# Summing three operands instead of four in phases 4 to 9 of an attention-and-MoE kernel, with the joined additions shared by VectorE and GpSimd

## The chip, the cores and the metric

One Trainium2 chip, one core. The metric is the device time of one execution in microseconds (us); before the change the median of three runs is 819.66 us (819.66 to 819.79).

## What is computed

A clustered attention is followed by two feed-forward layers. Queries and keys of 2 x 8 heads (768 rows of 64) are each assigned to the nearest of 16 centroids; a query sees the keys of its own cluster alone.

```python
mask = q_assign[:, :, :, None] == k_assign[:, :, None, :]
scores = scale * np.matmul(q, k.transpose(0, 1, 3, 2))
scores = np.where(mask, scores, -1000000000.0)
scores = scores - np.max(scores, axis=-1, keepdims=True)
attn = np.exp(scores)
attn = attn / (np.sum(attn, axis=-1, keepdims=True) + 1e-09)
return np.matmul(attn, v).astype(np.float32)
```

The result, 1536 rows of 512, goes through `h = x @ w_in` (512 to 2048) with a leaky rectifier and `@ w_out`, and then through a gated layer with RMS normalization (512 to 1536 and back). The change touches the attention alone: the sum over the keys in the denominator, and how one operand of the scores is split.

## The kernel before

**Phases and slots.** The attention is done by pairs of heads (`pr`, 0 to 7). Each pair has two phases (`ph`, 0 to 15), one for each half of its 768 queries; a phase has six slots, one for each tile of 128 keys, so that phase `ph` starts at slot 6 ph. In a slot TensorE makes the scores of 128 keys x 384 queries for both heads (`st_tile`, L712 and L713, transposed: keys lie on the partitions), and ScalarE takes their exponential into a tile P of 128 x 2 x 384 (L714). Every second slot, `pv_tiles` multiplies the last two tiles with the values (L728).

**The denominators.** They are sums of P over the keys, hence over partitions, and so a product with a matrix of ones into the bank `ps_sm` (L739): four small matmuls per tile of P, one for each head and half of the queries, each into 32 rows of the bank. A fp32 matmul stands in the trace as two entries, so that one operand is 8 entries of L739. In phases 4 to 12 (`SUMMED`) TensorE doesn't sum all six tiles of P: VectorE adds the first two and the next two (`pair_add`, L747, 128 x 768), and the last call of `pv_tiles` in the phase, at the slot after its end, sums what is in the list `adds` and the last two tiles of P. That is four operands. In the phases of the table `WHOLE`, 10 and 11 before the change, `pair_join` (L751) also adds the two sums to one, so that three operands are left; there the joined one is taken last (`q = P + self.adds`), elsewhere the additions come first.

**The maxima, nine slots ahead.** For the softmax, the score product is also made with queries on the partitions (`max_tile`, L662), in two halves into the single banks `ps_ma` and `ps_mb`, each reduced by VectorE to one column (L664). TensorE may write a bank again when VectorE has reduced it. At the end of a phase's six tiles the maxima of the two halves are joined (L681) and split in a rounded part and the rest (L671, L672, `max_split`); TensorE turns them into rows (`max_rows`, L690), and ScalarE copies these into the operand of the scores (L699).

**Preparing the pairs.** For each pair, some 40 slots ahead and by the tables `PAIR`, `FIFTH` and so on (slots counted from the pair's first one, 12 pr): squares of q and k (L469), their sums (L483), the norms by three Newton steps (`prep_norm`, L435 to L442, VectorE, tiles of 128 x 24), similarities and argmax (L543 to L565), and the split of q and k in a rounded part (`hi`, L606, ScalarE, 128 x 768) and a residual (`lo`, L614: for q by VectorE, for k of pairs 4 to 7 by GpSimd). The pairs 0 to 4 have tables of their own; `FIFTH` (pair 4) takes `hi` from `PAIR` and has a `lo` of its own.

**The output of a phase.** One to twelve slots after its end: reciprocals (L757 to L769), their split by GpSimd (L774, L775), the product X (L787, VectorE), its rounding (`x1h`, L795, ScalarE) and its residual (`x1l`, L798, GpSimd). The weights of the feed-forward layers are decoded in the same slots from slot 59 on.

**What sets the order.** `plan` puts every step into a slot with a number that orders it inside the slot, and `slot` issues the steps of a slot in that order. So each engine has a fixed queue and no step overtakes another on its engine; between engines only the data's waits count. `at(s, o, fn, ...)` is the call: slot, number, step.

```python
def at(s, o, fn, *a):
    ev.setdefault(s, []).append((o, len(ev.get(s, [])), fn, a))
```

Of the kernel before, what the change touches and what calls it, by code (L numbers as in the profile page):

```python
# [13 lines left out]
ALU = mybir.AluOpType  # L14
# [9 lines left out]
    "sq": ((-38, 4), (-36, 1.015)),  # L24
    "ss": ((-37, 0.6), (-36, 2.05)),
    "norm": tuple((t, 5 + n / 100) for n, t in enumerate([-32] + [-31] * 6 + [-30] * 7)),
    "hi": ((-28, 1.06), (-27, 1.06)),
    "lo": ((-24, 2.3), (-25, 1.05)),
    "sims": ((-30, 1.6), (-29, 1.7)),
    "scale": ((-29, 1.75),),  # L30
    "arg": ((-27, 5), (-24, 2.1), (-24, 2.2), (-22, 1.62), (-21, 5)),
# [57 lines left out]

SUMMED = range(4, 13)  # L90
FULL = (4, 6, 8, 10)
WHOLE = {10: (6, 1.99), 11: (5, 0.59)}
SQUARED = 2
ASIDE = (2,)
NEWTON = (2, 3)
# [130 lines left out]
class Attention:  # L226
# [489 lines left out]
    def pv_tiles(self, u):  # L716
# [13 lines left out]
        if ph in SUMMED and t0 < T - 2:  # L730
            self.addends[u] = P
            return
        q = P + self.adds if ph in WHOLE else self.adds + P
        self.adds = []
# [11 lines left out]
        self.adds.append(a)  # L746
        self.nc.vector.tensor_tensor(out=a, in0=P[0], in1=P[1], op=ALU.add)  # L747

    def pair_join(self):
        a, b = self.adds  # L750
        self.nc.vector.tensor_tensor(out=a, in0=a, in1=b, op=ALU.add)  # L751
        self.adds = [a]

    def out_first(self, ph):
# [45 lines left out]
    def plan(self):  # L800
# [3 lines left out]
        def at(s, o, fn, *a):  # L804
            ev.setdefault(s, []).append((o, len(ev.get(s, [])), fn, a))
# [4 lines left out]
        for pr in range(self.NP):  # L810
            b = SLOTS * pr
# [24 lines left out]
        for ph in range(NF):  # L836
            b = T * ph
            last = ph == NF - 1
            slots = AHEAD.get(ph, [b + k - LEAD for k in range(T)])
            for k, s in enumerate(slots):  # L840
                early = s < 0 or s % 2 and (s > 15 or ph < DIRECT and (s == 15 or slots.count(s) > 1))
                if s >= STEADY and not early:
                    at(s, 1.01, self.max_tile, ph, k, (0,))
                    at(s, 1.03, self.max_tile, ph, k, (1,))
                else:
                    at(s, 2.7 if s in slots[:k] else 0.5 if early else 1.5, self.max_tile, ph, k)
            mid, end = slots[T // 2 - 1], slots[-1]
            if ph < DIRECT:
                at(mid, 1.6, self.max_split, ph, 0)
                at(mid + 1 if ph else mid + 2, 1.8 if ph else 0.6, self.max_rows, ph, 0)  # L850
                last_rows = 1.01 if ph == DIRECT - 1 else 0.7
                at(end, 1.45 if end % 2 and end > 0 else 1.6, self.max_split, ph, 1)
                at(end + 1, last_rows, self.max_rows, ph, 1)
            else:
                at(end, 1.6, self.max_split, ph, None)
                at(end + 1, 0.7, self.max_rows, ph, None)
                at(end + 1, 0.71, self.rows_copy, ph, (0,))
                at(end + 1, 1.01, self.rows_copy, ph, (1,))
            for t in range(T):
                for e in range(2):  # L860
                    ahead = ((-7, 0.6), (-7, 0.7), (-5, 1))[t] if ph == e == 0 and t < 3 else ()
                    at(*(ahead or (b + t, 1 + e / 50)), self.st_tile, b + t, e)
                if t % 2:
                    at(b + t + 1, 2, self.pv_tiles, (b + t) // 2)
                    if ph in SUMMED and t < T - 1:
                        late = ph in FULL and t == 1
                        at(b + t + 1 + late, 1.1 if late else 2, self.pair_add, (b + t) // 2)
            if ph in WHOLE:
                at(b + WHOLE[ph][0], WHOLE[ph][1], self.pair_join)
            calm = STEADY <= b + 7 and not last  # L870
            at(b + (7 if calm else 6), 0.6 if calm else 3, self.out_first, ph)
            at(b + 6, 2.1, self.out_evac, ph)
            at(b + 7, -0.5 if last else 1.025, self.out_recip, ph)
            at(b + 7, -0.4 if last else 1.75, self.out_parts, ph)
            at(b + (8 if last else 10), -0.3 if last else 1.7, self.out_bcast, ph)
            at(b + (8 if last else 10), -0.2 if last else 1.75, self.out_mult, ph)
            soon = ph % 2 == 0 and ph < NF - 2
            at(b + (8 if last else 11 if soon else 12), -0.1 if last else 0.9 if soon else 1.04, self.out_split, ph, 0)
            at(b + (8 if last else 11 if soon else 12), 0 if last else 0.95 if soon else 1.05, self.out_split, ph, 1)
# [495 lines left out]
```

## Time and profile before

| | |
|---|---|
| Median of 3 runs | 819.66 us (819.66 to 819.79) |
| The profiled execution, its time | 819.63 us |
| Its span, from the first to the last instruction | 817.9 us |
| TensorE matmul (PE) | 809.6 us busy, 99% of the span |
| VectorE (DVE) | 623.7 us, 76% |
| ScalarE (ACT) | 335.6 us, 41% |
| GpSimd (POOL) | 362.1 us, 44% |
| TensorE clock granted | 1.0 of full speed in every slice |

The attention takes roughly the first 260 us; phases 4 to 9 lie between 92 and 176 us. They fill the fifth to the ninth of the page's forty slices, and VectorE's busy digit is 9 in each of these; in the second half of the kernel it falls to 7 and below. A busy time counts an instruction from start to end, so that neighbours overlap by some 0.08 us on VectorE and by half of their length on TensorE; what an instruction costs its queue is read from one start to the next. The idle time in brackets is the engine's own, with the instruction that ended it.

### The profile page before, as it was taken

The page shows a single profiled execution, that of the slowest core. Times are in us where ns is not written, and L with a number is a line of the kernel's source. Part 1 is how long each engine was busy: PE and PEld are TensorE (multiplying, and loading weights), DVE is VectorE, ACT ScalarE, POOL GpSimd, SP SyncE. Part 2 cuts the span into 40 slices and gives each one's busy share as a digit, 9 for nine tenths or more (in the row PEclk, how much of TensorE's full clock was granted, in tenths as well). Part 3 has the DMA queues.
Part 4 walks back from the last instruction along what each step waited for, and adds up shares of the span by engine and source line. Part 5 has one row for each costly group of instructions (what it writes and reads, how often), then busy time and mean ns, then how long its engine had stood idle before and what let it go on. Part 6 is the DMA issues. An engine that isn't in the chain of part 4 may idle for free.

```text
span 817.9 us, 11705 instructions
## 1 busy us (share of the span) xinstructions
PE 809.6 (99%) x4350; PEld 625.0 (76%) x4350; DVE 623.7 (76%) x1036; ACT 335.6 (41%) x652; POOL 362.1 (44%) x335
## 2 busy tenths in 40 slices
PE   8999999999999999999999999999999999999998
PEld 5565666666666888888888888888888888888887
DVE  6989999999998489999999977877555555555523
ACT  7655776666564333433434444432212221222110
POOL 3421221221213267786766772416465546554511
PEclk9999999999999999999999999999999999999999
DMA  8786655754532022232212220102121212121012
GB/s 206 201 229 181 132 154 161 171 111 115 133 114 79 1 77 78 78 103 65 88 59 75 77 78 1 51 1 78 52 77 54 76 52 77 57 73 51 1 52 103
DMA packets 23624, 74.03 MB, mean 91 GB/s; under 512 B 3600, under 2 KB 4752, under 8 KB 23568
## 3 DMA queue, kind: packets, MB, share of 16 engines
q1 hardware_dynamic: 23568, 73.29, 31.3%
q8 instruction: 34, 0.56, 0.3%
q14 instruction: 22, 0.18, 0.1%
HBM read 49.88 MB, written 3.15 MB: 65 GB/s over the span
## 4 chain that ended last, share of the span: by engine, by line
PE 96%; DVE 2%; DMA 1%; ACT 1%; issue 0%; SPq 0%; DVEq 0%; ACTq 0%
PE ps_st L1010 35%; PE ps_mx L1010 14%; PE ps_pv L1010 14%; PE ps_pv L728 8%; PE ps_pr L1010 5%; PE ps_st L712 4%; PE ps_st L713 4%; PE ps_sm L739 3%; PE ps_ma L662 3%; PE ps_mb L662 2%; DMA nat<-in_kn_dram 1%; DVE mx L666 1%; PE ps_pv L393 1%; PE ps_pr L516 1%; PE ps_pr L690 0%; PE ps_pr L782 0%
## 5 line engine op out<-in xcount | busy, mean ns | idle before, releaser
L1077 POOL TENSOR_TENSOR gl<-v,gh 128x512 fp32r<-128x512 f32 x68 | 96.0, 1412 | 143.8 <-ACT gh L1076 142.4
L1076 ACT CAST gh<-v 128x512 fp32r<-128x512 f32 x68 | 42.3, 622 | 151.9 <-DVE v L1073 83.3
L1073 DVE TENSOR_TENSOR v<-ps_st,t 128x512 f32<-128x512 f32 x36 | 24.9, 691 | 100.3 <-PE ps_st L1010 100.2
L714 ACT ACTIVATE p<-ps_st 128x384 f32<-128x384 f32 x192 | 85.3, 491 | 28.1 <-PE ps_st L713 26.6
L992 DVE SCALAR_TENSOR_TENSOR dec_a<-raw,dec_a 128x512 uint32<-128x512 uint32 x66 | 81.6, 1236 | 2.2
L728 PE MATMUL ps_pv<-p,vnat 128*64 128x384 f32 x384 | 72.6, 499 | 0.0
L1069 DVE SCALAR_TENSOR_TENSOR v<-v,alpha,t 128x512 f32<-128x512 f32 x45 | 53.0, 1177 | 21.9 <-ACT v L1068 21.8
L712 PE MATMUL ps_st<-op 128*128 128x384 f32 x192 | 67.8, 353 | 0.3 <-ACT oht L575 0.3
L1010 PE MATMUL ps_st<-x1h,stage 128*128 128x512 f32 x272 | 67.2, 389 | 0.0
L713 PE MATMUL ps_st<-op 82*128 82x384 f32 x192 | 65.0, 339 | 0.0
L1010 PEld LDWEIGHTS ps_st<-x1h,stage 128*128 128x128 f32 x272 | 51.1, 188 | 10.6
L1123 DVE TENSOR_TENSOR x<-ps_mx,x 128x1024 f32<-128x1024 f32 x36 | 43.9, 1220 | 18.7 <-PE ps_mx L1010 18.7
L664 DVE TENSOR_REDUCE mx<-ps_ma 128x1 f32<-128x384 f32 x90 | 49.7, 552 | 10.1 <-PE ps_ma L662 9.2
L798 POOL TENSOR_TENSOR x1l<-X,x1h 128x384 fp32r<-128x384 f32 x15 | 15.9, 1062 | 91.7 <-ACT x1h L795 91.7
L1010 PE MATMUL ps_st<-x1h,wvh 128*128 128x512 f32 x144 | 56.2, 390 | 0.0
L1010 PE MATMUL ps_st<-x1h,wvl 128*128 128x512 f32 x144 | 56.0, 389 | 0.0
L1010 PE MATMUL ps_st<-x1h,wih 128*128 128x512 f32 x132 | 51.6, 391 | 0.0
L1010 PE MATMUL ps_st<-x1h,wil 128*128 128x512 f32 x132 | 51.4, 389 | 0.0
L664 DVE TENSOR_REDUCE mx<-ps_mb 128x1 f32<-128x384 f32 x90 | 49.4, 549 | 0.1
L1123 DVE TENSOR_TENSOR x<-ps_pv,x 128x1024 f32<-128x1024 f32 x35 | 42.5, 1214 | 6.8 <-PE ps_pv L1010 6.8
L990 DVE TENSOR_SCALAR dec_a<-raw 128x512 uint32<-128x512 uint32 x66 | 47.6, 722 | 0.0
L995 DVE SCALAR_TENSOR_TENSOR dec_e<-raw,dec_e 128x512 f32<-128x512 uint32 x66 | 45.7, 692 | 2.3
(304 smaller groups left out, 1998.3 us busy)
## 6 DMA issues: line engine op xcount, KB each, us to landing
raw<-in_moe_w_out_dram SPq DMA_DIRECT2D x28, 512.0 KB, 3.5
op<-stage SPq DMA_DIRECT2D x32, 384.0 KB, 5.9
raw<-in_moe_w_in_dram SPq DMA_DIRECT2D x15, 512.0 KB, 3.6
raw<-in_moe_w_val_dram SPq DMA_DIRECT2D x12, 512.0 KB, 3.4
raw<-in_moe_w_gate_dram SPq DMA_DIRECT2D x12, 512.0 KB, 3.4
op<-stage SPq DMA_DIRECT2D x16, 288.0 KB, 5.9
raw<-in_qt_dram SPq DMA_DIRECT2D x8, 384.0 KB, 4.8
raw<-in_kt_dram SPq DMA_DIRECT2D x8, 384.0 KB, 5.1
```

What stands on the lines that cost most here:

```text
L664: nc.vector.tensor_reduce(out=mx[:, g, k:k + 1], in_=to, op=ALU.max, axis=AX.X)
L712: nc.tensor.matmul(ps, lhsT=o1[:, 1, ks], rhs=o1[:, 0, qs], start=True, stop=False)
L713: nc.tensor.matmul(ps, lhsT=o2[:, 1, ks], rhs=o2[:, 0, qs], start=False, stop=True)
L714: nc.scalar.activation(out=self.P[s][:, e], in_=ps, func=AF.Exp, scale=self.scale)
L728: nc.tensor.matmul(ps[64 * e:64 * e + 64], lhsT=self.vnat[ph // 2][:, e, t0 + y], rhs=P[y][:, e], start=t0 + y == 0, stop=t0 + y == T - 1)
L990: lambda: v.tensor_scalar(out=a, in0=top, scalar1=3, scalar2=0x3FFFFFFF, op0=ALU.logical_shift_left, op1=ALU.bitwise_and),
L992: lambda: v.scalar_tensor_tensor(out=a, in0=top, scalar=0xC0000000, in1=a, op0=ALU.bitwise_and, op1=ALU.bitwise_or),
L995: lambda: v.scalar_tensor_tensor(out=ef, in0=bot, scalar=2.0 ** -52, in1=ef, op0=ALU.mult, op1=ALU.mult),
L1010: self.nc.tensor.matmul(ps, lhsT=a, rhs=b, start=first and i == 0, stop=last and i == len(terms) - 1)
L1069: nc.vector.scalar_tensor_tensor(out=v, in0=v, scalar=self.nalpha[:, a], in1=t, op0=ALU.mult, op1=ALU.add)
L1077: nc.gpsimd.tensor_tensor(out=lo, in0=v, in1=f(hi), op=ALU.subtract)
L1123: nc.vector.tensor_tensor(out=dst, in0=ps, in1=dst, op=ALU.add)
```

## The change

Three tables and one step change.

- `WHOLE` gets the phases 4 to 9: in the even ones the join stands in the phase's sixth slot with the number 5, in the odd ones in the fifth slot with 2.5, right after the second `pair_add`. The denominators of these phases are then summed over three operands, the joined one last.
- `pair_join` takes the phase: in phases 5, 7 and 9 GpSimd adds, in the others VectorE.
- `hi` in `PAIR` (pairs 4 to 7): the second rounding, that of k, goes from slot -27 to slot -28, right behind the first.
- `lo` in `PAIR` (pairs 5 to 7): GpSimd's residual of k goes from slot -25 to slot -27.

```diff
--- before.py
+++ after.py
@@ -24,8 +24,8 @@
     "sq": ((-38, 4), (-36, 1.015)),
     "ss": ((-37, 0.6), (-36, 2.05)),
     "norm": tuple((t, 5 + n / 100) for n, t in enumerate([-32] + [-31] * 6 + [-30] * 7)),
-    "hi": ((-28, 1.06), (-27, 1.06)),
-    "lo": ((-24, 2.3), (-25, 1.05)),
+    "hi": ((-28, 1.06), (-28, 1.07)),
+    "lo": ((-24, 2.3), (-27, 0.9)),
     "sims": ((-30, 1.6), (-29, 1.7)),
     "scale": ((-29, 1.75),),
     "arg": ((-27, 5), (-24, 2.1), (-24, 2.2), (-22, 1.62), (-21, 5)),
@@ -89,7 +89,7 @@
 
 SUMMED = range(4, 13)
 FULL = (4, 6, 8, 10)
-WHOLE = {10: (6, 1.99), 11: (5, 0.59)}
+WHOLE = {**{ph: ((5, 5), (4, 2.5))[ph % 2] for ph in range(4, 10)}, 10: (6, 1.99), 11: (5, 0.59)}
 SQUARED = 2
 ASIDE = (2,)
 NEWTON = (2, 3)
@@ -746,9 +746,9 @@
         self.adds.append(a)
         self.nc.vector.tensor_tensor(out=a, in0=P[0], in1=P[1], op=ALU.add)
 
-    def pair_join(self):
+    def pair_join(self, ph):
         a, b = self.adds
-        self.nc.vector.tensor_tensor(out=a, in0=a, in1=b, op=ALU.add)
+        (self.nc.gpsimd if ph % 2 and ph < 10 else self.nc.vector).tensor_tensor(out=a, in0=a, in1=b, op=ALU.add)
         self.adds = [a]
 
     def out_first(self, ph):
@@ -866,7 +866,7 @@
                         late = ph in FULL and t == 1
                         at(b + t + 1 + late, 1.1 if late else 2, self.pair_add, (b + t) // 2)
             if ph in WHOLE:
-                at(b + WHOLE[ph][0], WHOLE[ph][1], self.pair_join)
+                at(b + WHOLE[ph][0], WHOLE[ph][1], self.pair_join, ph)
             calm = STEADY <= b + 7 and not last
             at(b + (7 if calm else 6), 0.6 if calm else 3, self.out_first, ph)
             at(b + 6, 2.1, self.out_evac, ph)
```

How it moves the instructions, first on VectorE at the end of phase 4 (L664 reduces the maxima, L437 and L429 are Newton steps of pair 5; one piece of the difference):

```order
 L664 TENSOR_REDUCE mx<-ps_ma 128x1
 L664 TENSOR_REDUCE mx<-ps_mb 128x1
+L751 TENSOR_TENSOR add_1414<-add_1414,add_1447 128x768
 L437 TENSOR_SCALAR n_y<-n_a 128x24
 L429 TENSOR_TENSOR n_a<-n_y,ss_1280 128x24
```

The join goes in between the reductions and the Newton steps; the same piece comes again in phases 6 and 8.

On GpSimd, from the output steps of phase 4 to those of phase 6, before (L775 splits reciprocals, L798 is the residual of an output, L614 the residual of k of pair 5):

```order
L775 TENSOR_TENSOR hl<-rs,hl 128x192
L798 TENSOR_TENSOR x1l<-X,x1h 128x384
L614 TENSOR_TENSOR stage_106<-raw_1237,stage_106 128x768
L774 TENSOR_SCALAR hl<-rs,low 128x192
L775 TENSOR_TENSOR hl<-rs,hl 128x192
```

and with the change:

```order
L775 TENSOR_TENSOR hl<-rs,hl 128x192
L614 TENSOR_TENSOR stage_106<-raw_1237,stage_106 128x768
L751 TENSOR_TENSOR add_1584<-add_1584,add_1637 128x768
L798 TENSOR_TENSOR x1l<-X,x1h 128x384
L774 TENSOR_SCALAR hl<-rs,low 128x192
L775 TENSOR_TENSOR hl<-rs,hl 128x192
```

The residual of k now stands ahead of the output's, with the join behind it; so in the phases 7 and 9 as well.

On TensorE, the sum of phase 4, before (L728 is the product with the values, L516 belongs to the similarities):

```order
L516 MATMUL ps_pr<-raw_1237,cb 32x384 x4
L728 MATMUL ps_pv<-p,vnat 64x384 x4
L739 MATMUL ps_sm<-add_1414,ones 32x192 x4
L739 MATMUL ps_sm<-add_1447,ones 32x192 x4
L739 MATMUL ps_sm<-p,ones 32x192 x8
L662 MATMUL ps_ma<-op_3_118 128x384
```

and with the change:

```order
L516 MATMUL ps_pr<-raw_1237,cb 32x384 x4
L728 MATMUL ps_pv<-p,vnat 64x384 x4
L739 MATMUL ps_sm<-p,ones 32x192 x8
L739 MATMUL ps_sm<-add_1414,ones 32x192 x4
L662 MATMUL ps_ma<-op_3_118 128x384
```

Four matmuls go, and the tiles of P come ahead of the joined sum.

## Rows read from the trace of the kernel before

**Rows 1.** The page: the chain that ended last, share of the span by engine.

```profile
PE 96%; DVE 2%; DMA 1%; ACT 1%; issue 0%; SPq 0%; DVEq 0%; ACTq 0%
```

**Rows 2.** The chain's pieces, sums of phases 4, 6, 10: start, duration, engine, tile, line, count.

```profile
104.70 1.44 PE ps_sm L739 x32
...
132.92 1.44 PE ps_sm L739 x32
...
188.15 1.11 PE ps_sm L739 x24
```

**Rows 3.** Timeline, VectorE, phase 4's end: start, duration, engine, line, operation [idle before <-releaser].

```profile
102.47 0.18 DVE L431 SCALAR_TENSOR_TENSOR n_y<-n_a,n_y 128x24 f32<-128x24 f32 x1
...
103.94 0.41 DVE L431 SCALAR_TENSOR_TENSOR n_y<-n_a,n_y 128x24 f32<-128x24 f32 x1
...
106.55 0.56 DVE L664 TENSOR_REDUCE mx<-ps_ma 128x1 f32<-128x384 f32 x1 [0.78 <-PE ps_ma L662]
```

**Rows 4.** Timeline, VectorE and TensorE, last slot of phase 6.

```profile
129.12 0.56 DVE L664 TENSOR_REDUCE mx<-ps_ma 128x1 f32<-128x384 f32 x1
...
129.73 0.44 PE L662 MATMUL ps_ma<-op 80*128 80x384 f32 x1
...
130.01 0.34 PE L712 MATMUL ps_st<-op 128*128 128x384 f32 x1
```

**Rows 5.** Timeline, VectorE, third slot of phase 5 (slot 32).

```profile
109.92 0.17 DVE L671 TENSOR_SCALAR mh<-mx 128x6 fp32r<-128x6 f32 x1
110.12 0.17 DVE L672 SCALAR_TENSOR_TENSOR mh<-mx,mh 128x6 fp32r<-128x6 f32 x1
110.21 0.95 DVE L747 TENSOR_TENSOR add<-p 128x768 f32<-128x768 f32 x1
111.08 0.55 DVE L664 TENSOR_REDUCE mx<-ps_ma 128x1 f32<-128x384 f32 x1
```

**Rows 6.** Timeline, GpSimd, phases 2, 4 and 9.

```profile
74.42 1.00 POOL L798 TENSOR_TENSOR x1l<-X,x1h 128x384 fp32r<-128x384 f32 x1 [11.27 <-ACT x1h L795]
...
103.31 1.00 POOL L798 TENSOR_TENSOR x1l<-X,x1h 128x384 fp32r<-128x384 f32 x1 [7.83 <-ACT x1h L795]
...
172.34 1.82 POOL L614 TENSOR_TENSOR stage<-raw,stage 128x768 fp32r<-128x768 f32 x1
```

**Rows 7.** Timeline, VectorE, phase 2.

```profile
74.46 1.00 DVE L429 TENSOR_TENSOR n_a<-n_y,ss 128x24 f32<-128x24 f32 x1
75.49 0.18 DVE L430 SCALAR_TENSOR_TENSOR n_a<-n_a,n_y 128x24 f32<-128x24 f32 x1
...
77.82 0.30 DVE L442 RECIPROCAL n_a<-n_y 128x24 f32<-128x24 f32 x1
78.04 0.49 DVE L664 TENSOR_REDUCE mx<-ps_ma 128x1 f32<-128x384 f32 x1
```

**Rows 8.** Timeline, TensorE, slots 32 and 33.

```profile
108.10 0.34 PE L712 MATMUL ps_st<-op 128*128 128x384 f32 x1
...
110.61 0.34 PE L690 MATMUL ps_pr<-idr,mh 128*64 128x128 f32 x3
...
111.90 0.34 PE L662 MATMUL ps_ma<-op 80*128 80x384 f32 x1
```

**Rows 9.** Timeline, ScalarE, slots 32 and 33.

```profile
109.04 0.82 ACT L606 CAST stage<-raw 128x768 fp32r<-128x768 f32 x1
110.99 0.47 ACT L699 CAST op<-ps_pr 2x384 fp32r<-2x384 f32 x1 [1.13 <-PE ps_pr L690]
...
112.88 0.82 ACT L606 CAST stage<-raw 128x768 fp32r<-128x768 f32 x1
113.60 0.87 ACT L714 ACTIVATE p<-ps_st 128x384 f32<-128x384 f32 x2
```

**Rows 10.** Timeline, VectorE, phase 9.

```profile
173.70 0.87 DVE L555 TENSOR_TENSOR sims<-sims,am 128x384 f32<-128x384 f32 x1
...
176.48 0.56 DVE L664 TENSOR_REDUCE mx<-ps_ma 128x1 f32<-128x384 f32 x1 [0.45 <-PE ps_ma L662]
```

## The prediction

> **What bounds the kernel now.** I read the chain that ended last first: TensorE carries 96% of it [rows 1], so time is saved only where TensorE is given less to do and nothing makes it wait. Then I read the stretch of phases 4 to 9 engine by engine, to see how close VectorE runs behind. Phases come in pairs of 28.2 us (the sums of phases 4 and 6 start at 104.70 and 132.92) [rows 2]. VectorE stops once in a pair for long: 0.78 us before a maximum, after the sums of the even phase [rows 3]. And at one place in a pair TensorE already waits for VectorE: the reduction from 129.12 ends at 129.68, the next score product for ps_ma starts at 129.73, and the matmul behind it at 130.01 [rows 4]. So both engines are nearly full, and what matters is how far VectorE falls behind, not its average.
>
> **The sums.** A sum over four operands takes 1.44 us of the chain, one over three 1.11 us [rows 2]; six phases go from four to three: 6 x 0.33 = 1.98 us less for TensorE. The joined operand now comes last, so it is needed some 0.7 us later than the first. That is the whole gain: 819.63 - 1.98 = 817.65 if nothing waits.
>
> **The joins on VectorE (phases 4, 6, 8).** None stands there in the trace, but the same operation on the same shape does: from a pair's addition at 110.21 to the reduction behind it at 111.08, 0.87 us [rows 5]. The join goes in after the reductions of the phase's last slot, ahead of the Newton steps. The idle 0.78 us after the sums [rows 3] nearly covers it: alone it makes VectorE 0.1 us late.
>
> But it also moves the Newton steps by 0.87 us, and this I charge. The L431 that starts at 102.47 then starts at 103.34. GpSimd's residual of the output (L798) runs from 103.31 to 104.31 [rows 6], since ScalarE sets when, not VectorE. What happens then stands in phase 2: L429 started at 74.46, 0.04 us behind an L798 from 74.42, and took 1.00 us in place of 0.18, to the end of L798 [rows 6, 7]. Now L798 meets only the end of this stretch: L431 at 103.94 took 0.41 us, to 104.35 [rows 3]. So after the join the blocked step again ends at about 104.35, but with more still behind it. L430 then starts at about 104.6; from L430 to the reduction after the last Newton step phase 2 needs 78.04 - 75.49 = 2.55 us [rows 7]. That reduction starts at 107.15, not 106.55: VectorE is 0.60 us late, while TensorE is 0.33 us early. Bounds: 0.1 us late without the block; 0.9 us if L798 is waited for in full (0.1 + 1.00 - 0.23, the wait of L431 that goes away).
>
> **What TensorE does with it.** The reduction of 107.15 ends at 107.71, and the second matmul from there, as in [rows 4], starts 0.33 us after that: 108.04, against 108.10 before [rows 8]. The first saving is spent here, but for 0.06 us.
>
> **The second rounding (ScalarE).** It moves ahead of the copies of the maxima's rows, into 1.13 us in which ScalarE waits for TensorE; one rounding takes 0.72 us to the next start, 0.82 us in all [rows 9]. It costs ScalarE nothing. It would end at 109.04 - 0.06 + 0.72 + 0.82 = 110.52.
>
> **GpSimd's residual sooner (pairs 5 to 7, phases 5, 7, 9).** It now stands ahead of the join and of L798 in GpSimd's queue and takes 1.82 us [rows 6] as soon as that rounding is done, from 110.52 to 110.60. VectorE is then at the splitting of the maxima: L671 at 109.92 + 0.60 = 110.52, L672 at 110.72, the addition at 110.81 [rows 5]. The addition is long and would keep GpSimd out until its end, which would do no harm. But GpSimd asks before that: it comes in when L671 ends (110.69) and runs to 112.51. L672 has two inputs in SBUF, as L431 and L429 have, and a longer one, L555 at 173.70, was held up by just this residual (0.87 us, for 0.55, beside the one from 172.34) [rows 6, 10]. So L672 ends at 112.55, and the matmuls that turn the maxima (L690, 110.61 before [rows 8]) start at 112.6: TensorE stands for 2.0 us with nothing else in its queue. The addition is late by 2.3 us and holds up the next reduction; the product at 111.90 [rows 8] waits 0.1 us for it. So a pair costs between 2.0 us (TensorE) and 2.3 us (VectorE); I take 2.15. The second saving, of the odd phase, is lost where TensorE waits for VectorE already [rows 4].
>
> The Trainium skill (SBUF — State Buffer, "Who interferes with whom") says that a VectorE instruction with two SBUF inputs contends with a GpSimd instruction that reads SBUF, and that the first takes the port pair for all of its instruction. By that L672 waits, and the sum is the one below; no row here shows L672 beside L614, and by the rows of L798 alone it would be that of the third rival.
>
> **The joins on GpSimd (phases 5, 7, 9).** They read what VectorE's second addition leaves and run beside reductions, which have one input. Bounds: 1.82 us, as the residual of the same shape [rows 6], or somewhat more for an addition; the sum asks for it only two slots after that addition. I cost them at nothing; if one ran into L555, that would be 0.32 us more per pair [rows 10].
>
> **The sum.** 3 pairs x 2.15 = 6.45 us later. The saving of phase 9 stays, since VectorE idles 0.45 us before the reduction behind it [rows 10]: -0.33. So 819.63 + 6.45 - 0.33 = 825.75, say **825.7 us**; the median of the runs is 819.66, 0.03 us from the profiled execution. Its own range is 823.6 (one of three collisions misses) to 826.8 (each pair 0.32 us dearer).
>
> **Rivals.**
> 1. *TensorE alone counts* (17%): VectorE makes up each join in its idle time, no GpSimd instruction is in its way, 817.65 us, faster. For it: TensorE has 96% of the chain and the idle 0.78 us is there. Against it: the product at 111.90 starts only 0.27 us after the reduction from 111.08 ends (111.63) [rows 5, 8], less than the 0.33 us that TensorE gains; at 129.73 it is 0.05 us [rows 4]. It decides where VectorE gets ahead by 0.3 us per pair: so only if L431 loses its present 0.23 us of waiting and meets no new one.
> 2. *VectorE sets the pace, without a block* (13%): L798 gets its turn in another gap. The pair stays at 28.2 us, 0.1 us more or 0.15 us less, and only phase 9 keeps its saving: 819.63 - 0.33 and three times -0.14 to +0.09, so 818.9 to 819.6.
> 3. *Only L798 collides* (12%): the residual asks after the addition has started, that is, VectorE is under 0.35 us late or ScalarE 0.25 us later. At most 3 x 0.60 - 0.33 = +1.47: 821.1 us.
>
> That the edit is void is excluded: each sum loses four matmuls in the order shown above.
>
> **How the numbers follow.** The forecast has 58%. A measurement of this kernel tells 0.2% (1.64 us) from no change. Faster by more: rival 1, 0.17. Within: rivals 2 and 3, 0.25. Slower by more: the forecast, 0.58. The range takes in the forecast and rivals 2 and 3 (83%): 818.9 to 826.8; rival 1 is left out.
>
> **What would show it.** L739 down from 608 to 560 entries. Right: in phases 4, 6, 8 a Newton step of 0.8 to 1.0 us beside L798; in phases 5, 7, 9 an L672 (or L671, or an L747) of about 2 us beside L614, and TensorE idle for 2 us ahead of L690. Wrong: L672 at 0.17 us and the addition running when L614 comes; then the pair is 28.2 us (rival 2) or 27.5 us (rival 1). If L798 starts clear of the Newton steps, the first link is wrong.

## The result and the profile after

The change made the kernel slower: **828.52 us**, the median of five executions (826.82 to 828.65), against 819.67 (819.66 to 820.26) for the kernel before beside it; a ratio of 1.0095, 95% interval 1.0083 to 1.0106. The forecast was 825.7, its range ended at 826.8. The direction and the mechanism were right; a further cost, of the granted clock, was missed. The profiled execution took 828.53 us (before: 819.63), its span is 826.7 us, its mean TensorE clock 0.996 of full speed.

The page's chain by engine answers to [rows 1]:

```profile
PE 94%; DVE 4%; DMA 1%; ACT 1%; issue 0%; DVEq 0%
```

VectorE has twice its share (4% for 2%): the chain now runs through its late steps. Where the time went is read from the sums, the chain's pieces with start, duration, engine, tile, line and count. They answer to [rows 2]:

```profile
106.60 1.11 PE ps_sm L739 x24
136.75 1.11 PE ps_sm L739 x24
166.90 1.11 PE ps_sm L739 x24
183.81 1.11 PE ps_sm L739 x24
197.01 1.11 PE ps_sm L739 x24
```

These are phases 4, 6, 8, 9 and 10; each sum takes 1.11 us, as forecast. Phases 4, 6 and 10 of the kernel before stand in [rows 2]; its phases 8 and 9 are these:

```profile
161.12 1.44 PE ps_sm L739 x32
174.63 1.44 PE ps_sm L739 x32
```

The first sum is 1.90 us later than before, although the order of work differs only from some 80 us on. From there the pair of phases 4 and 5 takes 30.15 us in place of 28.22 (+1.93) and the next one 30.15 in place of 28.20 (+1.95). From the sum of phase 8 to that of phase 9 it is 16.91 us in place of 13.51 (+3.40), and from there to phase 10 13.20 in place of 13.52 (-0.32). Together +8.86 of the 8.90 us. So there are three things to explain: about 1.9 us per pair, 1.5 us more in the third, and 1.9 us ahead of all of them.

Two words for what follows: a *stand* is a time in which TensorE has nothing to do but wait for VectorE's L672, and a *fall* a stretch in which the clock granted to TensorE drops from 1.00 to 0.50 of full speed (2.4 to 1.2 GHz).

**The two collisions** lie where the prediction put them. The timeline of the changed kernel, VectorE, GpSimd and TensorE (start, duration, engine, line, operation, idle time before and what ended it), answers to [rows 3], [rows 5], [rows 6] and [rows 8]:

```profile
105.21 1.00 POOL L798 TENSOR_TENSOR x1l<-X,x1h 128x384 fp32r<-128x384 f32 x1 [7.83 <-ACT x1h L795]
105.24 1.01 DVE L431 SCALAR_TENSOR_TENSOR n_y<-n_a,n_y 128x24 f32<-128x24 f32 x1
...
109.04 0.49 DVE L664 TENSOR_REDUCE mx<-ps_ma 128x1 f32<-128x384 f32 x1
...
112.33 0.17 DVE L671 TENSOR_SCALAR mh<-mx 128x6 fp32r<-128x6 f32 x1
112.44 1.80 POOL L614 TENSOR_TENSOR stage<-raw,stage 128x768 fp32r<-128x768 f32 x1 [0.16 <-ACT stage L606]
112.54 1.73 DVE L672 SCALAR_TENSOR_TENSOR mh<-mx,mh 128x6 fp32r<-128x6 f32 x1
114.19 0.95 DVE L747 TENSOR_TENSOR add<-p 128x768 f32<-128x768 f32 x1
114.42 0.36 PE L690 MATMUL ps_pr<-idr,mh 128*64 128x128 f32 x3 [1.86 <-DVE mh L672]
```

L431 starts 0.03 us behind GpSimd's L798 and ends with it; L672 starts 0.10 us behind L614 and ends with it; TensorE stands for 1.86 us ahead of L690. The same happens again some 30.2 and 60.3 us later.

**The third stand is followed by a slow TensorE.** These are two stretches of the changed kernel by time: us, busy time of PE, PEld, DVE, ACT and POOL with counts, the granted clock, the DMA's share and GB/s. The first is the stand of the first pair and what follows, the second that of the third pair:

```profile
113.00:114.00 1.00, 0.00 (x0) 0.00 (x0) 1.00 (x1) 0.00 (x0) 1.00 (x1) 1.00 0.00 0
114.00:115.00 1.00, 0.58 (x5) 0.62 (x6) 1.00 (x2) 0.18 (x1) 0.24 (x1) 1.00 0.00 0
115.00:116.00 1.00, 1.00 (x8) 0.90 (x7) 1.00 (x4) 0.95 (x3) 0.00 (x0) 1.00 0.00 0
...
173.00:174.00 1.00, 0.00 (x0) 0.00 (x0) 1.00 (x1) 0.00 (x0) 1.00 (x1) 1.00 0.00 0
174.00:175.00 1.00, 0.28 (x3) 0.31 (x4) 1.00 (x2) 0.00 (x0) 0.54 (x1) 0.84 0.00 0
175.00:178.00 3.00, 3.00 (x12) 3.00 (x11) 2.17 (x5) 2.29 (x5) 0.00 (x0) 0.50 0.00 0
```

TensorE works at 1.00 right after the first stand. After the third, equally long, it is granted 0.50 (1.2 GHz) for three microseconds, with 12 matmuls in three microseconds, where above 8 went into one. This is what the third pair costs beyond the others: 16.91 us to the sum of phase 9, where 15.45 pass between the sums of the other pairs, 1.46 us more.

**The 1.9 us ahead of phase 4** are for the most part a low clock too, between 27 and 33 us (changed kernel, by time):

```profile
27.00:30.00 3.00, 2.97 (x11) 0.98 (x10) 2.80 (x8) 1.60 (x3) 2.61 (x7) 0.65 1.04 213
30.00:33.00 3.00, 3.00 (x25) 1.79 (x23) 1.63 (x3) 0.37 (x1) 2.23 (x6) 0.78 1.03 242
```

An estimate from these rows: 0.35 x 3 + 0.22 x 3 = 1.7 us of TensorE at full clock. TensorE's work in this stretch is the same in both kernels, and nothing shows that the low clock there comes from the change: the profile of experiment 2 below, a kernel as fast as the one before, has it as well (0.64 and 0.79), and the profiles of experiments 5 and 7 have a fall of the same kind somewhat sooner, between 18 and 23 us. In these four profiles the sum of phase 4 starts between 105.96 and 106.53 us by TensorE's timeline, in the eight without such a fall between 104.50 and 105.43; the kernel before, at 104.63, is one of the early ones, so part of the 1.9 us is the ordinary scatter of the beginning. Nor is the unchanged kernel free of low clocks: 10 of its 56 executions beside the experiments have a mean clock of 0.998 and took 820.88 to 823.47 us, the others 0.999 or 1.000 and 819.16 to 820.55. The five executions of the change fit a fall more or less: three near 828.5 us with a mean clock of 0.996, two near 826.85 with 0.998. Which of the falls it was in those without a profile is not on record.

### The profile page after: what moved, and what is told of

It reads as the page before. It is cut to its first block, busy times and chain, and to the rows that moved or that the text cites. A ratio compares the mean times of both kernels' runs of the same rounds, so it can differ in the third digit from the quotient of the medians.

```text
span 826.7 us, 11621 instructions
## 1 busy us (share of the span) xinstructions
PE 812.9 (98%) x4302; PEld 625.4 (76%) x4302; DVE 632.0 (76%) x1039; ACT 335.8 (41%) x652; POOL 366.9 (44%) x338
## 4 chain that ended last, share of the span: by engine, by line
PE 94%; DVE 4%; DMA 1%; ACT 1%; issue 0%; DVEq 0%
PE ps_st L1010 34%; PE ps_mx L1010 14%; PE ps_pv L1010 13%; PE ps_pv L728 7%; PE ps_pr L1010 5%; PE ps_st L712 4%; PE ps_st L713 4%; PE ps_sm L739 3%; PE ps_ma L662 3%; PE ps_mb L662 2%; DVE mx L664 1%; DMA op<-oht 1%; PE ps_pr L516 1%; DVE mh L672 1%; DVE mx L666 1%; PE ps_pv L393 1%
## 5 line engine op out<-in xcount | busy, mean ns | idle before, releaser
L728 PE MATMUL ps_pv<-p,vnat 128*64 128x384 f32 x384 | 73.8, 506 | 0.0
L664 DVE TENSOR_REDUCE mx<-ps_ma 128x1 f32<-128x384 f32 x90 | 49.3, 548 | 9.7 <-PE ps_ma L662 8.8
L664 DVE TENSOR_REDUCE mx<-ps_mb 128x1 f32<-128x384 f32 x90 | 49.2, 547 | 0.3 <-PE ps_mb L662 0.2
L798 POOL TENSOR_TENSOR x1l<-X,x1h 128x384 fp32r<-128x384 f32 x15 | 15.9, 1057 | 74.2 <-ACT x1h L795 74.2
```

The costliest lines, as they stand in the source:

```text
L664: nc.vector.tensor_reduce(out=mx[:, g, k:k + 1], in_=to, op=ALU.max, axis=AX.X)
L728: nc.tensor.matmul(ps[64 * e:64 * e + 64], lhsT=self.vnat[ph // 2][:, e, t0 + y], rhs=P[y][:, e], start=t0 + y == 0, stop=t0 + y == T - 1)
```

## Experiments

The first four runs tell the collisions from two other reasons. "Collision theory" is the prediction's; "load theory" says that VectorE is simply given too much; "GpSimd theory" blames the joins on GpSimd.

**1. The joins on VectorE alone**, phases 4, 6, 8; rounding and residual where they were.

```diff
-    "hi": ((-28, 1.06), (-28, 1.07)),
-    "lo": ((-24, 2.3), (-27, 0.9)),
+    "hi": ((-28, 1.06), (-27, 1.06)),
+    "lo": ((-24, 2.3), (-25, 1.05)),
-WHOLE = {**{ph: ((5, 5), (4, 2.5))[ph % 2] for ph in range(4, 10)}, 10: (6, 1.99), 11: (5, 0.59)}
+WHOLE = {**{ph: (5, 5) for ph in (4, 6, 8)}, 10: (6, 1.99), 11: (5, 0.59)}
```

> Joins in phases 4, 6, 8 only (VectorE), GpSimd's residual and the second rounding where they were before. Collisions theory: L431 stands 1.0 us beside L798 three times, but L672 takes 0.17 us since no L614 is ahead of it; VectorE is 0.6 us late per pair and no more: 820 to 821.4 us, clock 1.0. Load theory (0.87 us more for a full VectorE is the cost, wherever it stands): over 825 us. GpSimd theory (its joins and its new order cost the time): 818.7 to 819.7 us.

Measured: 821.19 us, median of 11 (before: 819.79, median of 35 executions beside the first four runs), ratio 1.0016 [1.0007, 1.0024]. L431 takes 1.01 us in all three phases (the first at 104.14), no L672 over 0.22. A pair takes 28.58 us, 0.36 more than before, though TensorE has 0.33 us less to do. So the join ahead of the Newton steps, with the first collision that it brings, costs about 0.7 us and eats the saving twice over.

**2. The joins on GpSimd alone**, phases 5, 7, 9, with both moves.

```diff
-WHOLE = {**{ph: ((5, 5), (4, 2.5))[ph % 2] for ph in range(4, 10)}, 10: (6, 1.99), 11: (5, 0.59)}
+WHOLE = {**{ph: (4, 2.5) for ph in (5, 7, 9)}, 10: (6, 1.99), 11: (5, 0.59)}
```

> Joins in phases 5, 7, 9 only (GpSimd), with the moved residual and rounding. Collisions theory: L431 stays at 0.41 us, VectorE isn't late, its addition L747 has begun when L614 comes, so L672 takes 0.17 us and TensorE doesn't stand: 818.6 to 819.7 us. Load theory: the same, 818.6 to 819.7 us. GpSimd theory: 824 us or more.

Measured: 819.6 us, ratio 0.9993 [0.9984, 1.0003]; no L672 over 0.24 us, pairs of 28.22. The joins on GpSimd and the moves cost nothing by themselves: with VectorE not late, L672 is done before L614 asks.

**3. Only the two moves**, no join at all (`WHOLE` as before, `hi` and `lo` as in the change).

> No joins in phases 4 to 9, only the moved residual and rounding. Collisions theory: L614 begins behind the start of L747, nothing waits: 819.3 to 820.0 us. If the moved residual meets L672 by itself, without VectorE being late: over 823 us.

Measured: 819.82 us, ratio 1.0001 [0.9993, 1.001], L672 at most 0.24 us, pairs of 28.21. No effect.

**4. The joins on VectorE behind six Newton steps.** All of the change, but in the even phases the join stands behind the slot's Newton steps and not ahead of them, so that these keep their time.

```diff
-WHOLE = {**{ph: ((5, 5), (4, 2.5))[ph % 2] for ph in range(4, 10)}, 10: (6, 1.99), 11: (5, 0.59)}
+WHOLE = {**{ph: ((5, 5.9), (4, 2.5))[ph % 2] for ph in range(4, 10)}, 10: (6, 1.99), 11: (5, 0.59)}
```

> The change, with VectorE's join behind the six Newton steps of its slot instead of ahead of them. Collisions theory: the Newton steps keep their time and L798 falls into the join and the reductions behind it; L431 at 0.2 to 0.4 us, VectorE late by 0.1 us at most, L672 at 0.17 us: 818.3 to 819.7 us, clock 1.0 in phases 4 to 9. Load theory: as the change, over 826 us, since VectorE does just as much.

Measured: **818.94 us**, ratio 0.999 [0.9982, 0.9999]: well below the change, and 0.85 us below the kernel before, barely clear of the noise, with as many instructions on every engine as the change. Its timeline, VectorE and GpSimd:

```profile
103.46 0.18 DVE L429 TENSOR_TENSOR n_a<-n_y,ss 128x24 f32<-128x24 f32 x1
103.67 0.18 DVE L430 SCALAR_TENSOR_TENSOR n_a<-n_a,n_y 128x24 f32<-128x24 f32 x1
103.78 0.95 DVE L751 TENSOR_TENSOR add<-add,add 128x768 f32<-128x768 f32 x1
104.08 1.51 POOL L798 TENSOR_TENSOR x1l<-X,x1h 128x384 fp32r<-128x384 f32 x1 [7.82 <-ACT x1h L795]
...
110.63 0.17 DVE L672 SCALAR_TENSOR_TENSOR mh<-mx,mh 128x6 fp32r<-128x6 f32 x1
110.71 0.95 DVE L747 TENSOR_TENSOR add<-p 128x768 f32<-128x768 f32 x1
111.10 2.27 POOL L614 TENSOR_TENSOR stage<-raw,stage 128x768 fp32r<-128x768 f32 x1 [0.74 <-ACT stage L606]
```

Now the long additions start first, and it is GpSimd that waits: L798 takes 1.51 us (1.00 alone), L614 2.27 (1.80). TensorE waits for neither. The Trainium skill (SBUF — State Buffer, "Who interferes with whom") says that whoever issues first has the shared ports for its whole instruction; these rows agree, in the other direction than those of the change. Load theory is refuted: the same load, 9.6 us less. Of the saving of 1.98 us, 1.31 show between the sums of phases 4 and 10 (82.14 us by TensorE's timeline, before 83.45): the even phases keep theirs and phase 9 too, from the sums of phases 5 and 7 to the next ones it is 0.06 and 0.10 us more than before, where TensorE waited for VectorE already [rows 4].

The next runs are about the rest: three times 1.95 us, less the 0.3 saved in phase 9, are not 8.9. The kernel before beside them took 820.29 us (11 executions; 820.27 in 10 beside the last two).

**5. TensorE kept at work in the third stand**: eight matmuls of zeros just ahead of that L690.

```diff
-        for t, o, n in WARMS:
+        for t, o, n in (*WARMS, (57, 0.69, 8)):
```

> The change with eight more matmuls of the zero tile in TensorE's queue just ahead of the third pair's L690, so that TensorE works through most of the 1.86 us for which it stood there; VectorE's and GpSimd's queues are as in the change. Theory A (TensorE's standing lowers its clock afterwards): L672 is held as before (1.7 us) and L690 starts at the same distance, but the granted clock of the 5 us behind it is 1.00 and not 0.5 to 0.84; from the sum of phase 8 to that of phase 9 15.4 to 15.7 us, not 16.9; 825.2 to 827.2 us in all. Theory B (the low clock at that place has nothing to do with the stall, or comes from the load): it falls as in the change, the distance is 16.7 to 17.1, 826.8 to 828.7 us.

Measured, ratio 1.0117 [1.0094, 1.014]: the place itself as theory A had it, the time not. From the sum of phase 8 to that of phase 9 it is 15.51 us, at a clock of 1.00, with L672 held for 1.76 us as before. But the median is 829.9 us (825.57 to 833.83), above what either theory had named: in the profiled execution the clock fell behind the first and the second stand (18.52 and 17.02 us from the sum of the even phase to that of the odd one), and once early, between 18 and 23 us. One of its six executions, with a mean clock of 1.000, took 825.57. My expectation took for granted that the falls stay where the first profile had them.

**6. The residual put back for the third pair alone**, so that the third L672 meets nothing.

```diff
+            if pr == 7:
+                tab = {**PAIR, "lo": ((-24, 2.3), (-25, 1.05))}
```

> The change with GpSimd's residual put back in GpSimd's queue, behind the join and L798, for the third pair alone. Collision theory with the clock: the third L672 takes under 0.25 us, TensorE no longer stands before its L690, so its clock stays at 1.00 behind it: from the sum of phase 8 to that of phase 9 13.4 to 13.9 us, not 16.9, and 823.2 to 825.5 us in all. Collision without the clock (the clock falls there anyway): 14.8 to 15.4 us, 824.8 to 827.2. GpSimd-join theory (the join beside VectorE makes the delay, the residual's place is no matter): 15.4 or more, and 826.8 or more.

Measured: 829.78 us (828.35 to 830.23), ratio 1.0112 [1.0097, 1.0126], again more than expected. At the third place itself it went as collision theory with the clock had it: no L672 over 0.25 us, no low clock, 13.88 us from the sum of phase 8 to that of phase 9. But the residual put back is not free: behind the join it starts only at 183.73, beside VectorE's L557, which is held for 2.08 us in place of 0.56, and TensorE waits 0.89 us for the reduction behind it. From the sum of phase 9 to that of phase 10 it is 14.66 us in place of 13.20. From the sum of phase 8 to that of phase 10 this makes 28.54 us; with a stand and no fall it would be 28.65 (15.45 + 13.20). One collision has taken the place of another. The two stands that were left were both followed by a fall. The first fall is as long as the longest seen, that behind the first stand of experiment 5 (by time, columns as above):

```profile
113.00:114.00 1.00, 0.84 (x6) 0.87 (x7) 1.00 (x3) 0.43 (x1) 0.00 (x0) 0.82 0.00 0
114.00:120.00 6.00, 6.00 (x20) 3.84 (x19) 3.72 (x7) 3.60 (x8) 1.30 (x1) 0.50 0.00 0
120.00:121.00 1.00, 1.00 (x5) 1.00 (x5) 0.58 (x2) 0.00 (x0) 1.00 (x2) 0.77 0.00 0
```

From the sum of phase 4 to that of phase 5 it is 18.51 us here and 15.44 in the profile of the change, where that stand had no fall: a fall of over six microseconds costs 3.07 us.

**7. The residual put back for all three pairs** (`lo` as in the kernel before, joins and `hi` as in the change).

> The change with GpSimd's residual put back in its queue in all three pairs; joins and the second rounding's place as in the change. Collision theory: L431 beside L798 still takes 1.0 us, no L672 is over 0.25 us, a pair takes 28.2 to 28.6 us, not 30.15; the clock does not fall in phase 9; 819.5 to 821.5 us. GpSimd-join or load theory: a pair takes 29.5 us or more, 824 us or more.

Measured: 825.21 us (824.75 to 826.43), ratio 1.0064 [1.0052, 1.0076], pairs of 29.67 and 29.70 us. I had expected 28.2 to 28.6, and that the joins on GpSimd cost nothing; this was wrong, and both numbers lie where the expectation put the other theories. Experiment 4 excludes load theory; what the joins on GpSimd do is seen in the rows. No L672 is held, but now the residual is, by the join ahead of it. The timeline, GpSimd and VectorE:

```profile
116.84 1.83 POOL L751 TENSOR_TENSOR add<-add,add 128x768 f32<-128x768 f32 x1 [5.10 <-PE ps_mb L662]
118.64 1.00 POOL L798 TENSOR_TENSOR x1l<-X,x1h 128x384 fp32r<-128x384 f32 x1
119.60 1.82 POOL L614 TENSOR_TENSOR stage<-raw,stage 128x768 fp32r<-128x768 f32 x1
120.20 1.64 DVE L555 TENSOR_TENSOR sims<-sims,am 128x384 f32<-128x384 f32 x1
...
123.82 0.44 PE L662 MATMUL ps_ma<-op 80*128 80x384 f32 x1 [1.16 <-DVE mx L664]
```

In experiment 1, without the join, L614 started at 117.83 and L555 took 0.54. Behind the join it starts at 119.60, runs into L555 and holds it for 1.1 us, and TensorE stands 1.16 us. So the join on GpSimd is free in the change only because the residual was taken out from behind it. No clock fell behind these shorter waits in this profile; its one fall is early, between 18 and 23 us.

**8. The change once more**, unaltered.

> The change once more, unaltered, for the two drops of the granted clock. If the drop at 27 to 33 us comes by chance and the one behind the third stall with the stall, the times lie in two groups 1.6 to 1.9 us apart, near 826.8 and 828.6 us, and the distance from the sum of phase 8 to that of phase 9 is 16.7 to 17.1 us in the profile whether the early drop is there or not. If the drop in phase 9 comes by chance as well, there are times near 825.3 too, or a profile in which that distance is 15.4 to 15.7.

Measured: 828.62, 826.52, 828.57 and 830.12 us, clocks of 0.996, 0.998, 0.996 and 0.994; ratio 1.0101 [1.0088, 1.0114]. In its profile there is no early fall. The falls are behind the first and the third stand: 16.91 and 16.90 us to the sum of the odd phase, behind the second stand 15.44. So the third stand is not special, and the grouping I expected (early fall by chance, the one in phase 9 always behind the stand) holds only in its first half: with experiments 5 and 6, each of the three stands has been followed by a fall. And 828.6 us comes about in more than one way, here with two falls behind stands and no early one.

**9. All joins on GpSimd**, VectorE with three instructions of 0.94 us less.

```diff
-        (self.nc.gpsimd if ph % 2 and ph < 10 else self.nc.vector).tensor_tensor(out=a, in0=a, in1=b, op=ALU.add)
+        (self.nc.gpsimd if ph < 10 else self.nc.vector).tensor_tensor(out=a, in0=a, in1=b, op=ALU.add)
```

> The change with the joins of phases 4, 6 and 8 on GpSimd too, ahead of L798 in its queue; VectorE has three instructions of 0.94 us less. Load theory (VectorE's own work sets the pace): no Newton step over 0.3 us, pairs of 27.6 to 28.0 us, 817.6 to 819.2 us. Collision theory: GpSimd's join, 1.8 us from the end of the second addition, holds one of VectorE's steps with two inputs (L429, L430 or L431) for 0.6 to 1.5 us in each of the three phases, and the L798 behind it comes about 0.5 us later than in the change and can hold another; VectorE is as late as in the change, within 0.5 us: 821 us or more, and 824 to 829 us where L672 is held beside L614 as well.

Measured: 827.88 us (826.48 to 833.5), ratio 1.0104 [1.0079, 1.0129]. Less work on VectorE, no time won. The timeline at the end of phase 4:

```profile
100.84 1.83 POOL L751 TENSOR_TENSOR add<-add,add 128x768 f32<-128x768 f32 x1 [5.50 <-DVE add L747]
101.69 1.01 DVE L437 TENSOR_SCALAR n_y<-n_a 128x24 int32<-128x24 int32 x1
103.17 1.00 POOL L798 TENSOR_TENSOR x1l<-X,x1h 128x384 fp32r<-128x384 f32 x1 [0.50 <-ACT x1h L795]
103.18 1.04 DVE L431 SCALAR_TENSOR_TENSOR n_y<-n_a,n_y 128x24 f32<-128x24 f32 x1
```

Two steps are held in place of one, and then L672 beside L614 (1.73 us) in all three pairs. I had named L429, L430 or L431; the first one held is L437, which has one input (0.16 us at 102.61 in experiment 4). The Trainium skill (SBUF — State Buffer, "Who interferes with whom") says that a tensor_scalar can enter a mode in which it uses both of VectorE's port pairs and then contends with GpSimd; this row agrees in that L437 ends with GpSimd's L751 (102.70 and 102.67), but no row shows in which mode it was.

**10. TensorE kept at work in all three stands**: the eight matmuls of experiment 5 at each place.

```diff
-        for t, o, n in WARMS:
+        for t, o, n in (*WARMS, *((s, 0.69, 8) for s in (33, 45, 57))):
```

> The change with eight matmuls of the zero tile ahead of the L690 of each of the three pairs, so that TensorE never stands there for the 1.86 us in which L672 is held; nothing else is altered, and L690 starts no sooner. Theory A (the standing lowers the clock): the clock stays at 1.00 behind all three places, the pairs take 30.0 to 30.3 us and from the sum of phase 8 to that of phase 9 it is 15.4 to 15.6 us; nearly all executions lie at 825.0 to 826.0 us (up to 1.9 us more where the early drop of 27 to 33 us falls), with a mean clock of 0.998 or more. Theory B (the clock falls by the load or by chance): times as the change's, 826.5 to 830 us, clock 0.991 to 0.996.

Measured: **825.5 us** (825.01 to 825.94 in five executions, clocks of 0.999 and 1.000), ratio 1.006 [1.0047, 1.0074]: 24 useless matmuls more than the change, and some 3 us less, though still slower than the kernel before. The timeline, TensorE, VectorE and GpSimd at the first place:

```profile
110.69 2.00 PE L393 MATMUL ps_pr<-zero 128*128 128x512 f32 x8
110.75 1.84 POOL L614 TENSOR_TENSOR stage<-raw,stage 128x768 fp32r<-128x768 f32 x1 [0.16 <-ACT stage L606]
110.85 1.76 DVE L672 SCALAR_TENSOR_TENSOR mh<-mx,mh 128x6 fp32r<-128x6 f32 x1
...
112.76 0.38 PE L690 MATMUL ps_pr<-idr,mh 128*64 128x128 f32 x3
```

L672 is held as before and L690 starts no sooner. The clock at the three places and behind them, by time, columns as above:

```profile
112.00:114.00 2.00, 1.93 (x13) 1.41 (x12) 2.00 (x4) 0.80 (x2) 0.59 (x1) 1.00 0.00 0
114.00:118.00 4.00, 4.00 (x24) 2.89 (x23) 4.00 (x8) 3.42 (x9) 0.73 (x1) 1.00 0.00 0
142.00:144.00 2.00, 1.92 (x12) 1.44 (x12) 2.00 (x3) 0.60 (x2) 0.79 (x1) 1.00 0.00 0
144.00:148.00 4.00, 4.00 (x24) 2.80 (x23) 4.00 (x9) 3.42 (x8) 0.52 (x1) 1.00 0.02 4
...
174.00:175.00 1.00, 1.00 (x7) 0.90 (x7) 1.00 (x3) 0.95 (x3) 0.00 (x0) 1.00 0.00 0
175.00:178.00 3.00, 3.00 (x18) 1.91 (x17) 3.00 (x7) 1.85 (x5) 0.31 (x1) 1.00 0.00 0
```

It is 1.00 in all three pairs, and from the sum of the even phase to that of the odd one it is 15.50, 15.49 and 15.51 us. This is the run that settles the cause of the falls in phases 4 to 9: with the collisions in place and TensorE's idleness alone removed, they go. Over all profiles with the collision, 8 of 13 stands left empty were followed by a fall, and none of the 4 that were filled. The clocks of all executions agree: all nine of the change have a mean clock of 0.998 or less, all five of this run 0.999 or 1.000.

## Why the prediction was wrong at the end and right before it

- *The sums*: right, 1.11 us each.
- *The joins on VectorE*: right. L431 is held for 1.01 us beside L798, in all three phases, the reduction behind the Newton steps comes 0.59 us later behind the sum of phase 4 than before (0.60 forecast), and the first saving is gone. Alone (experiment 1) the pair is 0.36 us longer, within the 0.60 that the third rival gave it.
- *The second rounding*: right, nothing (experiment 3).
- *GpSimd's residual sooner*: right in place and kind. L614 comes in as L671 ends, L672 is held for 1.73 us, TensorE stands 1.86 us. The pair costs 1.93 and 1.95 us where no fall follows, 1.99 and 2.01 in experiment 10 (30.21 us both, with 28.22 and 28.20 before, by TensorE's timeline); I took 2.15, between 2.0 and 2.3. The lower bound was nearer: the stand is 1.86 us where the forecast had 2.0, and what VectorE is late beyond it does not show in the pair.
- *The joins on GpSimd*: nothing in this order of work, but experiment 7 shows a condition: with the residual behind them it runs into L555.
- *What the Trainium skill says of the shared ports* (SBUF — State Buffer, "Who interferes with whom"): the collision of L672 with L614, which no row of before showed, is there as stated, 1.73 us in place of 0.17. The third rival (only L798 collides) is refuted.
- **The sum** is the step that failed. It priced each of the three pairs at 2.15 us: every term counted a wait as long as it lasts, with TensorE at full clock after it. The granted clock behind the stand stood in no term. The runs show it: a pair without a fall costs 1.93 to 2.01 us, a little less than forecast, but one with a fall of some three microseconds 3.40 (1.46 more), and a fall of over six microseconds adds 3.07. Where TensorE is kept at work in the stands, the sum holds: between the sums of phases 4 and 10 experiment 10 is 5.69 us longer than the kernel before, and the forecast had 6.12. That its 825.5 us lie so near to 825.7 is in part luck, since the kernel before ran at 820.27 beside it.
- *The range* ended at 826.8 us, by the wait's own bounds; a bound for the clock was wanted. Of the nine executions of the change one lies within it (826.52), one at 826.82, the others above. In the first profile the miss takes two falls: with +1.93, +1.95, +3.40 and -0.32 alone the time would be 826.6 us, still inside, and it is the 1.9 us ahead of phase 4, mostly the early fall, that carry it out. The early fall was in no term either, and it is not shown to be the change's. But the range fails without it as well: experiment 8's profile, 828.62 us, has 0.56 us ahead of phase 4 and then +3.40, +1.95, +3.39 and -0.32, from falls behind two stands.

Left open: which of the three equal stands is followed by a fall in an execution, and how long it lasts; why experiments 5 and 6, with one stand less, had more or longer falls than the change; and what sets off the early one.

## What to carry to other kernels

Price a wait of the engine that bounds the kernel twice: for its length, and for the clock that may be granted after it; where the wait can't be removed, useless matmuls in it can win back the second part, as they did here (828.5 to 825.5 us). Before an instruction is put on a busy engine, look at what stands behind it and what the engine that it collides with does just then: here the same join cost 0.7 us or won time, by where in the slot it stood. Where two engines hold each other up, order the work so that the one is held that nobody waits for: in experiment 4 it was GpSimd, at no cost.

## What was not expected of the hardware

- TensorE's clock fell to 0.50 (1.2 GHz) behind stands of only 1.86 us with TensorE at work before and behind them, in 8 of 13 cases over five profiles; equal stands were followed by 1.00 in the other 5.
- A step of 128 x 6 elements, 0.17 us alone, takes 1.73 us beside an operation of GpSimd, and an integer step of 128 x 24 with one input, 0.16 us alone, takes 1.01.
- Coming 0.10 us behind is enough to wait for the whole of the other engine's instruction: L672 from 112.54 ended with the L614 of 112.44. In experiment 4 L672, from 110.63, was through before L614 came at 111.10, and it was L614 that waited, for the addition behind L672.
